# Smaller, chained GpSimd loads, key tiles zeroed by VectorE, and head pairs in the order 0, 3, 1, 2

## The chip, the cores and the metric

The kernel runs on one core of one Trainium2 chip. The metric is the device time of the whole program in microseconds (us). The kernel before takes 461.84 us, the median of three runs (461.19 to 462.41).

## The reference

Two layers follow one another. The first is a gated linear recurrence over 768 time steps for 4 batches and 8 heads of 48 channels, the second a gated two-layer product with a shift by one time step. Cut to what matters:

```python
mag = np.sqrt(a_re * a_re + a_im * a_im)
scale = np.minimum(mag, 0.999) / (mag + 1e-06)
a_re_n, a_im_n = (a_re * scale, a_im * scale)
for t in range(S):                       # S = 768, states [B, H, D, D]
    new_re = ar * S_re - ai * S_im
    new_im = ar * S_im + ai * S_re
    S_re, S_im = (new_re + k[t] (x) v[t], new_im)
    y[t] = q[t] . S_re
...
xk = mu_k * x + (1 - mu_k) * x_prev      # x: y with the heads side by side, 384 wide
xr = mu_r * x + (1 - mu_r) * x_prev
k = np.maximum(xk @ w_k, 0.0)            # 1024 wide
v = k * k @ w_v
out = sigmoid(xr @ w_r) * v
```

## The kernel before, in words

The 4 x 768 time steps are cut into 8 units of 384 steps, two for each batch (u = 0 to 7; an odd unit goes on from the state of the even one ahead of it). Each unit goes through three stages, called G, A and M here:

- **G(u)**, `gate` (L637): GpSimd loads one tile `g` of 128 x 3 x 4 x 384 numbers (three blocks of 128 channels, `ct`; in each a_re, a_im, k and q) and three tiles `v`. Unit 0's `g` is loaded by SyncE. ScalarE and VectorE then turn a_re and a_im into running logarithms and angles (L684 to L772), scale k and q (L740), and turn them by cosine and sine (L784). For unit 0 the work is done in two groups of blocks, (0) and (1, 2); for the others in one group. There are two buffers for `g`, five for `v`.
- **A(u)**, `attend` (L800): SyncE's transfers (`move`, L816) put the keys and queries of a head under each other in one of six tiles `kq`, whose rows between the real and the imaginary part hold zeros that are written once at the start (L351). TensorE multiplies keys with queries per chunk of 128 steps (`scores`, `sc`, L885), VectorE masks the product (`pt`, L889), TensorE transposes keys (`tr`, L847), updates the state (`up`, L867) and forms the outputs for pairs of heads (`y`, L908 and L915). ScalarE copies them out (`ys`, L924) and SyncE's transfers bring them into the tile `xt` (L930): pairs 0, 1 and 2 go to rows 0 to 95 of block 0, 1 and 2, pair 3 to rows 96 to 127 of all three blocks.
- **M(u)**, `mix` (L384): VectorE forms the difference of neighbouring steps (`dx`, L396) and the two mixed inputs (L405 or L415), for units other than 0 also split into a high and a low part (L423, L426). TensorE multiplies (`z`, L439 for unit 0 with whole weights, L444 for the others), ScalarE applies relu, square (L484, L488), VectorE splits again (L496), TensorE multiplies with the second weight (`o`, L512 or L515), VectorE multiplies with the sigmoid (L534) and SyncE stores. A product `z` needs all three blocks of the mixed input.

The weights come once, ten loads by GpSimd (`raw`, L363), and are decoded on ScalarE and VectorE (L578 to L588). Nineteen later loads (`again`, L627) read them a second time for a check of their range. GpSimd also copies the last step of an even unit (`last`, L947), which the odd unit's M needs.

The order of all this is written by a planner inside the kernel, the class `Plan` (L70). Every step is registered with an engine, an estimated cost, what it reads and writes, and which buffers it uses. The table `AT` (L44) gives each stage A and M a start and an end on a common scale; TensorE's steps are ordered by it and their costs added up, and each step gets a due time by walking back from those through what it feeds (`due`, L117). `run` (L156) then plays the engines forward in its own time: whenever an engine is free, it takes the step with the earliest due time among those that can start. The order so found is the order of instructions of each engine, and on the chip no engine leaves it. SyncE's transfers ("SP") and GpSimd's loads ("GP") are engines of the plan with a time per issue (`QUEUE`), and each had a data path of its own with its own rate (L325, L329). GpSimd's compute steps are booked on another engine of the plan, "POOL", though on the chip they share one stream with its loads. The line that says when transferred data is there is

```python
dma[e] = max(dma[e], t + self.START) + cost     # START 1.15, cost bytes by rate
end = dma[e] + self.ARRIVE                      # ARRIVE 0.9
```

and the head pairs are walked in the order of `PAIRS` (L46): the transfers of a pair, then its scores, then its outputs. While TensorE waits for the first M, `warm` (L962) fills it with products that nobody reads.

Of the kernel before, what the change touches and what calls it, by code (L numbers as in the profile page):

```python
# [11 lines left out]
F32 = mybir.dt.float32  # L12
# [18 lines left out]
HR = 64  # L31
# [9 lines left out]
CAP = 0.999  # L41


AT = ((0.38, 0.74), (1.0, 1.45), (1.28, 1.33), (2.34, 3.3), (2.2, 2.89), (3.4, 4.43), (3.07, 3.65), (4.24, 5.39),  # L44
      (4.34, 4.39), (4.94, 6.44), (5.25, 5.8), (7.11, 7.17), (6.14, 7.38), (7.41, 9.17), (7.2, 7.7), (9.54, 10.42))
PAIRS = 0, 1, 2, 3  # L46
PIECE = 2
GP = 2
KQ = 6
# [7 lines left out]
FIRST_LOAD = 2  # L57
# [12 lines left out]
class Plan:  # L70
# [8 lines left out]
    BEGIN = 0.8  # L79
    LATENCY = 0.16  # L80
    TABLE = 1.28
    QUEUE = dict(SP=0.63, GP=1.1)
    START, ARRIVE = 1.15, 0.9
    TURN = {("once", "half"): 0.09, ("full", "half"): 0.09,
            ("half", "once"): 0.24, ("half", "full"): 0.15}
# [70 lines left out]
    def run(self):  # L156
# [10 lines left out]
        ready = [0.0] * len(ops)  # L167
        tables = sorted(o["table"] for o in ops if o["table"])[::-1]
        table, end = None, 0.0
        dma = dict.fromkeys(self.QUEUE, 0.0)  # L170
        work = {}
        free, held, got = {}, dict.fromkeys(self.bufs, 0), dict.fromkeys(self.bufs, 0)
        taken, waiting, events, ends, order = set(), {}, [self.BEGIN], [], []
        warm = False
        kind = None

# [17 lines left out]
        while len(order) < len(ops):  # L194
            t = heapq.heappop(events) + 1e-9
            while ends and ends[0][0] <= t:
                for s in ops[heapq.heappop(ends)[1]]["uses"]:
                    users[s] -= 1
                    if not users[s]:
                        held[s[0]] -= 1  # L200
            found = True
            while found:
                found = False
                for e, queue in list(waiting.items()):
                    if free.get(e, 0.0) > t:
# [12 lines left out]
                    if self.fill and self.fill[3] in o["writes"]:  # L218
                        warm = False
                    for other in (o["engine"], *o["other"]):  # L220
                        waiting[other].discard(i)
                    if self.fill and self.fill[2] in o["writes"]:
                        warm = True
                    for tag, n in set(o["uses"]) - taken:
                        taken.add((tag, n))
                        held[tag] += 1
                        got[tag] = max(got[tag], n + 1)
                    cost = o["other"].get(e, o["cost"])
                    if o["table"]:
                        tables.pop()  # L230
                        if table != o["table"][1]:
                            table = o["table"][1]
                            cost += self.TABLE
                    if e in self.QUEUE:
                        free[e] = t + self.QUEUE[e]
                        dma[e] = max(dma[e], t + self.START) + cost
                        end = dma[e] + self.ARRIVE
                    else:
                        end = t + cost
                        if e == "PE":  # L240
                            end = t
# [29 lines left out]
def tile_kernel(ctx, tc, gat, vt, w_all, mu, slow_g, slow_v, out):  # L271
# [50 lines left out]

    def op_dma(n, f, **kw):

        plan[0].op("SP", n / 360, f, **kw)  # L325

    def op_dma_gp(n, f, **kw):

        plan[0].op("GP", n / 300, f, **kw)  # L329


    table(AF.Ln)
# [15 lines left out]

    kqs = [keep.tile([HR + D, 2, U], F32, name=f"kq{i}") for i in range(KQ)]
    for t in kqs:  # L350
        nc.gpsimd.memset(t[32:HR], 0.0)  # L351
    last = keep.tile([P, NT, 1], F32, name="last")
    nc.sync.dma_start(out=mu_sb, in_=mu)

# [188 lines left out]
    with ExitStack() as fast:  # L543
# [7 lines left out]
        slot = plan[0].slot  # L551
        G, g_slot, V, v_slot = {}, {}, {}, {}

        raws = {}

        def fetch(i):
            s = pieces[i]
# [79 lines left out]
        def gate(u):  # L637
# [6 lines left out]
            v_slot[u] = [slot("v") for _ in range(NC)]  # L644
            V[u] = []

            def load(ct, part):
                def f():
                    if u not in G:
                        G[u] = gp.tile([P, NT, 4, U], F32, tag="g", name="g")  # L650
                    (nc.gpsimd if u else nc.sync).dma_start(out=G[u][:, ct, part], in_=gat[b, half, ct, :, part])
                (op_dma_gp if u else op_dma)(196.6 * (part.stop - part.start), f, writes=[("g", u, ct, i) for i in range(part.start, part.stop)] + [("in", u, ct, part.stop)],
                       uses=[g_slot[u]])

            def load_v(c):
                def f():
                    v = ap.tile([P, C], F32, tag="v", name="v", bufs=5)
                    nc.gpsimd.dma_start(out=v, in_=vt[b, half, c])
                    V[u].append(v)
                op_dma_gp(197, f, writes=[("v", u, c)], uses=[v_slot[u][c]])  # L660

            def each(c):
                return range(c.start, c.stop)
# [126 lines left out]
                    op_dve(2 * U, lambda ct=ct: times(ct, 1), reads=[("r0", u, ct)],  # L790
                           writes=g[2:] + [("kqs", u, ct)], uses=[s_r, s_g])

            parts = (slice(0, 2), slice(2, 4)) if u < FIRST_LOAD else (slice(0, 4),)
            steps = [lambda ct=ct, part=part: load(ct, part) for part in parts for ct in cts]
            steps += [lambda c=c: load_v(c) for c in range(NC)]
            for f in (a0, a1, a2, b0, b1):
# [328 lines left out]
```

## Time and profile before

| | |
|---|---|
| median of three runs | 461.84 us |
| profiled execution | 460.59 us |
| its span, first to last instruction | 458.6 us |
| mean granted TensorE clock | 0.945 |
| bytes moved | 67.51 MB, 147 GB/s over the span |

An engine's idle time costs something only where TensorE, which does most of the work, ends up waiting for it. A row of a timeline gives start, duration, engine, source line, operation, output<-input, shape, count and, in brackets, the idle time before it with what ended that. A row of the windows gives busy time and, in parentheses, the count of instructions of each engine in a stretch, then the granted TensorE clock, the share of DMA time, and GB/s. "PEld" is TensorE's loading of weights. A row of the transfers gives their count, size and median time from issue to landing.

### The profile page before, as it was taken

The page shows a single profiled execution, that of the slowest core. Times are in us where ns is not written, and L with a number is a line of the kernel's source. Part 1 is how long each engine was busy: PE and PEld are TensorE (multiplying, and loading weights), DVE is VectorE, ACT ScalarE, POOL GpSimd, SP SyncE. Part 2 cuts the span into 40 slices and gives each one's busy share as a digit, 9 for nine tenths or more (in the row PEclk, how much of TensorE's full clock was granted, in tenths as well). Part 3 has the DMA queues.
Part 4 walks back from the last instruction along what each step waited for, and adds up shares of the span by engine and source line. Part 5 has one row for each costly group of instructions (what it writes and reads, how often), then busy time and mean ns, then how long its engine had stood idle before and what let it go on. Part 6 is the DMA issues. An engine that isn't in the chain of part 4 may idle for free.

```text
span 458.6 us, 8780 instructions
## 1 busy us (share of the span) xinstructions
PE 399.6 (87%) x3263; PEld 362.6 (79%) x3263; DVE 329.3 (72%) x536; ACT 341.6 (74%) x591; POOL 52.2 (11%) x116
## 2 busy tenths in 40 slices
PE   2005998999977999999999999999899998999994
PEld 2004995567666999999898989999799997899993
DVE  1599868669849988878886888777897866185222
ACT  5689755987768799989978799789879943563530
POOL 8510020000201120030003000011000000100000
PEclk8555999999978999999999999999999999999998
DMA  8996380602885827383647345268541455300001
GB/s 284 411 410 178 95 290 2 134 22 66 262 189 154 286 55 179 121 281 118 148 127 245 120 112 146 66 216 226 134 135 47 118 135 144 112 4 22 32 1 59
DMA packets 25074, 67.51 MB, mean 147 GB/s; under 512 B 5696, under 2 KB 11840, under 8 KB 25024
## 3 DMA queue, kind: packets, MB, share of 16 engines
q1 hardware_dynamic: 17520, 30.69, 25.6%
q0 software_dynamic: 7504, 36.18, 23.3%
q8 instruction: 28, 0.46, 0.4%
q14 instruction: 22, 0.18, 0.1%
HBM read 38.54 MB, written 4.72 MB: 94 GB/s over the span
## 4 chain that ended last, share of the span: by engine, by line
PE 56%; DMA 16%; ACT 10%; DVE 10%; issue 4%; SPq 2%; POOL 2%; DVEq 0%; ACTq 0%; POOLq 0%
PE z L444 18%; PE o L515 13%; PE sc L885 8%; DMA raw<-in_w_all 4%; DMA xt<-ys 4%; PE y L908 3%; PE o L512 3%; PE up L867 3%; DMA again<-in_w_all 3%; PE y L915 3%; PE z L439 3%; DMA kq<-g 3%; PE tr L847 2%; ACT r L295 2%; SPq L816 1%
## 5 line engine op out<-in xcount | busy, mean ns | idle before, releaser
L444 PE MATMUL z<-x,w 128*128 128x384 f32 x693 | 132.1, 340 | 0.0
L444 PEld LDWEIGHTS z<-x,w 128*128 128x128 f32 x693 | 120.6, 188 | 0.7 <-issue 0.7
L515 PE MATMUL o<-hhi,w 128*128 128x384 f32 x336 | 87.7, 342 | 0.0
L885 PE MATMUL sc<-kq 112*128 112x128 f32 x384 | 57.7, 297 | 5.8 <-DMA kq<-g 4.8
L515 PEld LDWEIGHTS o<-hhi,w 128*128 128x128 f32 x336 | 59.9, 188 | 0.6 <-issue 0.5
L885 PEld LDWEIGHTS sc<-kq 112*128 112x128 f32 x384 | 50.6, 204 | 11.0 <-issue 7.6
L515 PE MATMUL o<-hlo,w 128*128 128x384 f32 x168 | 57.1, 340 | 2.3 <-DVE hlo L496 2.2
L847 PE MATMUL tr<-ident,g 128*128 128x128 f32 x120 | 20.3, 298 | 36.2 <-DVE g L784 36.2
L847 PEld LDWEIGHTS tr<-ident,g 128*128 128x128 f32 x120 | 15.9, 153 | 39.3 <-DVE g L784 37.3
L484 ACT ACTIVATE r<-z 128x384 f32<-128x384 f32 x64 | 30.8, 483 | 20.6 <-PE z L444 20.0
L784 DVE TENSOR_TENSOR g<-g,r 128x768 f32<-128x768 f32 x48 | 43.1, 954 | 3.1 <-ACT r L295 2.9
L889 DVE TENSOR_TENSOR pt<-sc,mask 128x384 f32<-128x384 f32 x64 | 34.6, 552 | 5.4 <-PE sc L885 4.7
L515 PEld LDWEIGHTS o<-hlo,w 128*128 128x128 f32 x168 | 31.5, 188 | 3.9 <-DVE hlo L496 3.9
L423 ACT CAST x<-xm 128x384 fp32r<-128x384 f32 x42 | 21.1, 512 | 17.5 <-DVE xm L415 15.1
L488 ACT ACTIVATE h<-r 128x384 f32<-128x384 f32 x64 | 33.0, 520 | 0.8
L496 DVE TENSOR_TENSOR hlo<-h,hhi 128x384 fp32r<-128x384 f32 x56 | 30.9, 554 | 2.4 <-ACT hhi L311 1.0
L295 ACT ACTIVATE sq<-m 128x1152 f32<-128x1152 f32 (+2 forms) x27 | 28.0, 1054 | 6.1 <-DVE m L732 3.7
L908 PE MATMUL y<-pt,v 128*64 128x128 f32 (+1 forms) x384 | 29.3, 280 | 3.0 <-DVE pt L889 3.0
L311 DVE CAST hhi<-h 128x384 fp32r<-128x384 f32 x33 | 11.8, 358 | 25.9 <-PE o L515 13.4
L908 PEld LDWEIGHTS y<-pt,v 128*64 128x64 f32 (+1 forms) x384 | 20.8, 129 | 11.5 <-issue 5.8
L289 ACT ACT_TABLE_LOAD x22 | 28.2, 1283 | 1.2 <-PEq L1114 0.8
L627 POOL DMA_DIRECT2D again<-in_w_all x19 | 10.2, 539 | 161.9 <-ACT again L634 114.4
(85 smaller groups left out, 687.9 us busy)
## 6 DMA issues: line engine op xcount, KB each, us to landing
kq<-g SPq DMA_DIRECT2D x96, 144.0 KB, 3.4
g<-in_gat POOLq DMA_DIRECT2D x18, 768.0 KB, 6.4
again<-in_w_all POOLq DMA_DIRECT2D x19, 384.0 KB, 3.7
raw<-in_w_all POOLq DMA_DIRECT2D x9, 768.0 KB, 10.3
v<-in_vt POOLq DMA_DIRECT2D x24, 192.0 KB, 6.2
out_t<-y SPq DMA_DIRECT2D x24, 192.0 KB, 3.2
xt<-ys SPq DMA_DIRECT2D x48, 72.0 KB, 3.2
kq<-g SPq DMA_DIRECT2D x32, 96.0 KB, 3.1
```

Source lines behind the costliest of these rows:

```text
L289: nc.scalar.add_instruction(mybir.InstLoadActFuncSet(name=nc.get_next_instruction_name(), act_func_set_id=loaded[0], engine=mybir.EngineTy ...
L295: nc.scalar.activation(out=out, in_=in_, func=func, **kw)
L444: nc.tensor.matmul(z, lhsT=wt[s[0]][:, part, s[1]], rhs=r[which][:, ct], start=n == 0, stop=n == 3 * NT - 1)
L484: nc.scalar.activation(out=t["r", j], in_=t["f", j], func=AF.Relu)
L488: nc.scalar.activation(out=t["h", j], in_=t["r", j], func=AF.Square)
L496: nc.vector.tensor_tensor(out=t["lo", j], in0=t["h", j], in1=t["hi", j].bitcast(F32), op=ALU.subtract)
L515: nc.tensor.matmul(tiles["o", mt], lhsT=wt[W_V + 2 * j][:, part, ts(mt, P)], rhs=r, start=j == 0 and n == 0, stop=j == NJ - 1 and n == 2)
L784: nc.vector.tensor_tensor(out=g[:, ct, 2 * i:2 * i + 2], in0=g[:, ct, 2:4], in1=t["r"][:, ct, 1 - i:2 - i].to_broadcast([P, 2, U]), op=ALU ...
L847: nc.tensor.transpose(out=t["tr", c, part][:, ct * P:(ct + 1) * P], in_=G[u][:, ct, 2 * part, c * P:(c + 1) * P], identity=ident)
L885: nc.tensor.matmul(sc[:, c], lhsT=kq[h][:, 0, ts(c, P)], rhs=kq[h][:, 1, ts(c, P)], start=True, stop=True)
L889: nc.vector.tensor_mul(pts[h], t["sc", h], mask.unsqueeze(1).to_broadcast([P, NC, P]))
L908: nc.tensor.matmul(t["y", p][rows, ts(c, P)], lhsT=V[u][c][:, cols], rhs=pts[hs[j]][:, c], start=c == 0, stop=False)
```

## The change

Five things are changed together.

1. The loads of `g` come in two halves of 384 KB for every unit, first a_re and a_im of the three blocks, then k and q, where units 2 to 7 had one load of 768 KB for each block.
2. From unit 2 on, ahead of each load of `g` or `v`, GpSimd copies one number out of the tile loaded ahead of it (`touch`), and so waits until that load has landed. The planner is told of it (`reads=before(...)`).
3. The six tiles `kq` are zeroed by VectorE.
4. The planner's picture of the transfers is another: one data path for SyncE and GpSimd together, rates of 380 and 400 bytes per ns, 0.65 us per GpSimd issue, GpSimd free from 2.4 us on and VectorE from 5.5 us on.
5. `AT` and `PAIRS` have other values, so that the whole order is planned anew. In the old table A(1) lies inside M(0) and A(3) inside the end of M(1) and the start of M(2); in the new one A(1) comes after M(0), and A(2) and A(3) lie side by side in the second half of M(1).

```diff
-AT = ((0.38, 0.74), (1.0, 1.45), (1.28, 1.33), (2.34, 3.3), (2.2, 2.89), (3.4, 4.43), (3.07, 3.65), (4.24, 5.39),
-      (4.34, 4.39), (4.94, 6.44), (5.25, 5.8), (7.11, 7.17), (6.14, 7.38), (7.41, 9.17), (7.2, 7.7), (9.54, 10.42))
-PAIRS = 0, 1, 2, 3
+AT = ((1.08, 1.24), (1.06, 1.33), (1.56, 2.38), (2.41, 3.51), (2.81, 3.56), (4.05, 5.05), (2.79, 3.65), (4.94, 5.9),
+      (4.96, 5.14), (6.39, 7.0), (6.27, 6.51), (7.33, 8.26), (6.46, 8.29), (7.37, 12.32), (8.85, 9.08), (12.2, 12.46))
+PAIRS = 0, 3, 1, 2
...
-    QUEUE = dict(SP=0.63, GP=1.1)
+    QUEUE = dict(SP=0.63, GP=0.65)
+    FREE = dict(GP=2.4, DVE=5.5)
...
-                        dma[e] = max(dma[e], t + self.START) + cost
-                        end = dma[e] + self.ARRIVE
+                        dma = max(dma, t + self.START) + cost
+                        end = dma + self.ARRIVE
...
-        plan[0].op("SP", n / 360, f, **kw)
+        plan[0].op("SP", n / 380, f, **kw)
...
-        plan[0].op("GP", n / 300, f, **kw)
+        plan[0].op("GP", n / 400, f, **kw)
...
     for t in kqs:
-        nc.gpsimd.memset(t[32:HR], 0.0)
+        nc.vector.memset(t[32:HR], 0.0)
...
+            def after(key):
+
+                if loaded_by and u >= FIRST_LOAD:
+                    nc.gpsimd.tensor_copy(touch, loaded_by[-1])
+                loaded_by.append(key)
+
+            def before(key):
+                r = chain[-1:] * (u >= FIRST_LOAD)
+                chain.append(key)
+                return r
...
+                    if u:
+                        after(G[u][:1, ct, part.start, :1])
                     (nc.gpsimd if u else nc.sync).dma_start(out=G[u][:, ct, part], in_=gat[b, half, ct, :, part])
...
                     v = ap.tile([P, C], F32, tag="v", name="v", bufs=5)
+                    after(v[:1, :1])
                     nc.gpsimd.dma_start(out=v, in_=vt[b, half, c])
...
-            parts = (slice(0, 2), slice(2, 4)) if u < FIRST_LOAD else (slice(0, 4),)
+            parts = slice(0, 2), slice(2, 4)
```

More of the change, by code (lines that the diff above doesn't have):

```diff
@@ L169, in run @@
         table, end = None, 0.0
-        dma = dict.fromkeys(self.QUEUE, 0.0)
+        dma = 0.0
         work = {}
-        free, held, got = {}, dict.fromkeys(self.bufs, 0), dict.fromkeys(self.bufs, 0)
-        taken, waiting, events, ends, order = set(), {}, [self.BEGIN], [], []
+        free, held, got = dict(self.FREE), dict.fromkeys(self.bufs, 0), dict.fromkeys(self.bufs, 0)
+        taken, waiting, events, ends, order = set(), {}, [self.BEGIN, *self.FREE.values()], [], []
         warm = False
@@ L552, in tile_kernel @@
         G, g_slot, V, v_slot = {}, {}, {}, {}
-        raws = {}
+        raws, loaded_by, chain = {}, [], []
+        touch = keep.tile([1, 1], F32, name="touch")
         def fetch(i):
@@ L650, in f @@
                         G[u] = gp.tile([P, NT, 4, U], F32, tag="g", name="g")
+                    if u:
+                        after(G[u][:1, ct, part.start, :1])
                     (nc.gpsimd if u else nc.sync).dma_start(out=G[u][:, ct, part], in_=gat[b, half, ct, :, part])
-                (op_dma_gp if u else op_dma)(196.6 * (part.stop - part.start), f, writes=[("g", u, ct, i) for i in range(part.start, part.stop)] + [("in", u, ct, part.stop)],
-                       uses=[g_slot[u]])
+                key = ("in", u, ct, part.stop)
+                (op_dma_gp if u else op_dma)(
+                    196.6 * (part.stop - part.start), f, writes=[("g", u, ct, i) for i in range(part.start, part.stop)] + [key],
+                    reads=before(key), uses=[g_slot[u]])
             def load_v(c):
@@ L657, in f @@
                     v = ap.tile([P, C], F32, tag="v", name="v", bufs=5)
+                    after(v[:1, :1])
                     nc.gpsimd.dma_start(out=v, in_=vt[b, half, c])
                     V[u].append(v)
-                op_dma_gp(197, f, writes=[("v", u, c)], uses=[v_slot[u][c]])
+                op_dma_gp(197, f, writes=[("v", u, c)], reads=before(("v", u, c)), uses=[v_slot[u][c]])
             def each(c):
```

## The prediction

> **What bounds the kernel now.** I read the page first, then the busy times by stage, then for each stage where TensorE stands still the waits, the timeline and the chain.
>
> ```profile
> span 458.6 us, 8780 instructions
> PE 399.6 (87%) x3263; PEld 362.6 (79%) x3263; DVE 329.3 (72%) x536; ACT 341.6 (74%) x591; POOL 52.2 (11%) x116
> PE 56%; DMA 16%; ACT 10%; DVE 10%; issue 4%; SPq 2%; POOL 2%; DVEq 0%; ACTq 0%; POOLq 0%
> ```
>
> TensorE is the busiest engine, yet a sixth of the chain is transfers. The stretches say where; I cut them at the points where TensorE's work changes (start, A(0), the way to M(0), M(0) with A(1), A(2), the long middle).
>
> ```profile
> core 0: us, PE busy (x) PEld busy (x) DVE busy (x) ACT busy (x) POOL busy (x), PEclk, DMA share, GB/s
> 0.00:35.60 35.60, 2.93 (x12) 2.64 (x12) 20.26 (x32) 24.19 (x42) 17.90 (x44) 0.62 0.95 368
> 35.60:40.20 4.60, 0.48 (x2) 0.19 (x2) 4.57 (x8) 4.58 (x6) 0.00 (x0) 0.50 0.63 165
> 40.20:61.10 20.90, 20.90 (x259) 19.31 (x259) 18.97 (x28) 15.65 (x27) 2.02 (x4) 0.85 0.54 148
> 61.10:81.30 20.20, 18.24 (x104) 13.73 (x102) 13.73 (x21) 11.40 (x17) 1.77 (x4) 1.00 0.31 109
> 81.30:125.00 43.70, 43.67 (x309) 29.84 (x310) 35.18 (x44) 37.87 (x58) 3.19 (x6) 1.00 0.45 122
> 125.00:150.00 25.00, 18.71 (x214) 16.33 (x212) 16.67 (x30) 16.95 (x27) 2.12 (x4) 0.80 0.74 171
> 150.00:447.00 297.00, 289.85 (x2343) 276.07 (x2344) 216.73 (x374) 230.99 (x418) 25.17 (x55) 1.00 0.45 128
> ```
>
> From 150 us on TensorE is idle for 297.00 - 289.85 = 7.15 us in all: there it is the bound, and no order of the work brings more than that. What can be won lies in front: 40.2 us until TensorE's work starts, the way from A(0) to M(0), and 125 to 150, where it is idle for 6.29 us and the granted clock is 0.80 (by the clock alone 25.00 x 0.20 = 5.0 us more).
>
> **The start.** The waits and the timeline of the first 45 us:
>
> ```profile
> PE tr L847 <- DVE g L784: 34.9, 2, 30.8
> ```
>
> ```profile
> 2.27 4.11 POOL L351 MEMSET kq<- 32x768 f32 x6
> 4.47 0.52 ACT L684 ACTIVATE m<-g 128x384 f32<-128x384 f32 x1 [2.37 <-DMA g<-in_gat]
> 6.32 1.74 POOL L651 DMA_DIRECT2D g<-in_gat  x3
> 6.80 0.84 ACT L684 ACTIVATE m<-g 128x768 f32<-128x768 f32 x1 [1.09 <-DMA g<-in_gat]
> 8.18 0.56 DVE L690 SCALAR_TENSOR_TENSOR ph<-ph,g 128x384 f32<-128x384 f32 x1 [7.22 <-ACT ph L295]
> 15.73 0.56 ACT L578 ACTIVATE raw<-raw 128x384 int32<-128x384 uint8 x1 [5.02 <-DMA raw<-in_w_all]
> ```
>
> TensorE waits for G(0), and in the middle of G(0) ScalarE stands still for 5.02 us: the planner put the decoding of the first weights there because in its picture GpSimd's loads have a path of their own, and the weights came late. With one shared path they are expected later, and G(0)'s next steps take that place. I count 5.0 us off. Against it: GpSimd no longer zeroes the tiles (4.11 us), so its loads set out at about 2.3 instead of 6.32 us and share the path with unit 0's blocks 1 and 2, which land between 4.47 and 6.80 us; at half the rate these 2.33 us become 4.66, so at most 2.3 us later. I take 1.5, since the first half of that stretch passes before GpSimd's data flows. The zeroing on VectorE costs nothing: it has 7.22 us of idle time before 8.18, and six tiles of 768 columns take 3.3 to 5.7 us there by the two nearest rows of that width:
>
> ```profile
> L784 DVE TENSOR_TENSOR g<-g,r 128x768 f32<-128x768 f32 x48 | 43.1, 954 | 3.1 <-ACT r L295 2.9
> ...
> L732 DVE TENSOR_SCALAR m<-m 128x768 f32<-128x768 f32 x1 | 0.6, 554 | 0.0
> ```
>
> If that cover were gone it would be those us. **Term 1: -3.5 us** (bounds -5.0 and +2.3).
>
> **From A(0) to M(0).**
>
> ```profile
> 61.12 8.30 PE L966 MATMUL warm<-mask,ident 128*128 128x128 f32 x72
> 70.88 9.91 PE L439 MATMUL z<-x,raw 128*128 128x384 f32 x30 [1.45 <-issue]
> ```
>
> ```profile
> 67.88 0.56 DVE L396 TENSOR_TENSOR dx<-xt 128x384 f32<-128x384 f32 x1 [3.00 <-DMA xt<-ys]
> ...
> 70.17 1.67 DVE L405 SCALAR_TENSOR_TENSOR x<-dx,mu_sb,xt 128x384 f32<-128x384 f32 x3
> 71.75 2.83 DVE L751 TENSOR_TENSOR_SCAN ph<-ph,stat,consts 128x384 f32<-128x384 f32 x3
> ```
>
> ```profile
> 61.99 2.43 SPq L930 DMA_DIRECT2D xt<-ys  x4
> ```
>
> TensorE fills 8.30 us with products that nobody reads and is idle for 1.45, because all three blocks of `xt` wait for pair 3, the last: four transfers of 2.43 / 4 = 0.61 us each, then the differences and the mixed inputs of three blocks. In the order 0, 3, 1, 2 block 0 is whole after two pairs and block 1 after three; behind the last pair come two transfers and one block. That takes two transfers (1.2 us) and, for two blocks, 2 x (0.56 + 2 x 0.56) = 3.4 us of VectorE out of the way: 4.6 us, if VectorE does them under A(0), where it is busy for 18.97 of 20.90 us. I take 4.0. Less than nothing is hardly possible, as no step is added; the upper bound is the whole of 20.20 - 9.91 = 10.3 us, if G(1)'s scans (2.83 us, in the middle of that work) also move behind, which the later place of A(1) in the table favours. **Term 2: -4.0 us** (0 to -10.3).
>
> **The stall of A(2).**
>
> ```profile
> 115.29 1.58 POOL L651 DMA_DIRECT2D g<-in_gat  x3 [45.00 <-ACT r L772]
> ```
>
> ```profile
> 121.96 8.43 DMA kq<-g
> ```
>
> ```profile
> 128.78 3.31 PE L885 MATMUL sc<-kq 112*128 112x128 f32 x12 [3.46 <-DMA kq<-g]
> ```
>
> ```profile
> kq<-g SPq DMA_DIRECT2D x96, 144.0 KB, 3.4
> g<-in_gat POOLq DMA_DIRECT2D x18, 768.0 KB, 6.4
> again<-in_w_all POOLq DMA_DIRECT2D x19, 384.0 KB, 3.7
> ```
>
> The chain holds a transfer of keys of 8.43 us where the median is 3.4, and ahead of it stand G(3)'s three loads, issued in 1.58 us. Chained, one load of 384 KB is under way instead of 2.3 MB, and the transfer is 8.43 - 3.4 = 5.0 us earlier; TensorE's idle 6.3 us and the low clock, which follows it, shrink with that. Also in the new table M(1) stands ahead of A(2) and can fill. I take half of 6.3 + 5.0 = 11.3, since A(2)'s late readiness has a second cause, G(2)'s own end. **Term 3: -5.5 us** (0 to -11.3). A rule of the Trainium skill, DMA: Bandwidth & Descriptors, section Queues, rings and completion order, says that each DMA engine takes turns between the queues packet by packet; by it a bulk load of any size costs a transfer beside it half the rate and no more, so size alone would not help, only the pauses between the links. No row of this trace shows the turns.
>
> **The middle.** Of the 7.15 us from 150 on I take a fifth, as TensorE is the bound and other steps will be late instead. **Term 4: -1.5 us** (+3 to -7).
>
> **The chain of loads.** Each unit from 2 on has six loads of 384 KB and three of 192 KB one behind the other. A link takes issue to landing, 3.7 us for 384 KB by the row above and 3.2 for 192 KB by the stores, plus the copy of one number, at most the 0.9 us that a copy of `last`, three numbers in 128 rows, takes:
>
> ```profile
> out_t<-y SPq DMA_DIRECT2D x24, 192.0 KB, 3.2
> ```
>
> ```profile
> L947 POOL COPY last<-xt 128x3 f32<-128x3 f32 x4 | 3.6, 901 | 22.4 <-DMA xt<-ys 14.7 <-DMA kq<-g 6.4 <-issue 1.2
> ```
>
> 6 x 3.7 + 3 x 3.2 = 31.8 us, with the copies up to 31.8 + 9 x 0.9 = 39.9. What is there to cover it, in unit 4 of before:
>
> ```profile
> 147.87 1.58 POOL L651 DMA_DIRECT2D g<-in_gat  x3 [6.66 <-DMA out_t<-y]
> ```
>
> ```profile
> 165.34 1.17 ACT L684 ACTIVATE m<-g 128x1152 f32<-128x1152 f32 x1
> ```
>
> ```profile
> 185.10 2.17 PE L867 MATMUL up<-v,kt 128*64 128x48 f32 x64
> ```
>
> G(4) begins 17.5 us after its loads set out; the first three links, a_re and a_im, are there after 11.1 to 13.8 us. The last `v` is there after 31.8 to 39.9 us, and `up` wants it 185.10 - 147.87 = 37.2 us after the start: the cover is there, but used up to the edge. The planner books a link of 384 KB with 393 / 400 + 1.15 + 0.9 + 0.16 (its latency) = 3.2 us and one of 192 KB with 2.7, 27.3 us for nine; the rows say 31.8 and the copies, so that GpSimd runs 4.5 us or more behind its plan by the last link. Behind a waiting copy are queued, in GpSimd's one stream, the next loads of `g` and `v`, the loads of `again` (nobody but the range check waits for them) and the copy `last`, for which the odd unit's M waits. Six units of 31.8 us fit into the 300 us from 150 us on, so the path as a whole is not full. I charge 0.5 us for each of six units. **Term 5: +3.0 us** (0 to +27, below). A second rule of the Trainium skill, DMA: Bandwidth & Descriptors, section Rules for kernel authors, speaks against the change: at least 1 MiB for a transfer. By that page's fit, 2.0 us and the bytes at 436 GB/s, the nine links would take 6 x 2.9 + 3 x 2.45 = 24.8 us, an estimate, instead of 31.8; term 5 would then be near 0. The trace's link of 384 KB, 3.7 us, is slower than that fit.
>
> The rest has one answer: the count of steps, table loads and matmuls is the same, and the end behind the last product (unit 7's stores) is untouched.
>
> **Sum.** -3.5 - 4.0 - 5.5 - 1.5 + 3.0 = -11.5 us. The profiled execution took 460.59 us (its span and 2.0 us around it), so 449.1; it lies 1.25 us under the median of the runs, which makes 461.84 - 11.5 = **450.3 us**.
>
> **Rivals.**
>
> *VectorE bounds the start, and the gain is handed back.* For it:
>
> ```profile
> 20.00:30.00 10.00, 0.00 (x0) 0.00 (x0) 9.98 (x16) 9.21 (x16) 3.42 (x5) 0.50 1.02 412
> ```
>
> VectorE is full there; ScalarE's 5.02 us may only uncover that. Against it: much of what VectorE does in that stretch is decoding of weights, which has time until M(0). Terms 1 and 2 would be 0: 461.84 - 5.5 - 1.5 + 3.0 = **457.8 us**. Chance 0.13.
>
> *The transfers share anyway, so A(2) still stalls.* Keys and loads would move in turns whatever the size of a load. For it: the bytes are the same. Against it: three loads issued in 1.58 us keep the path full for most of the 8.43 us, a chained one, 0.39 MB at the 412 GB/s of the row above, for 0.96 of its 3.7 us. This is the rule of the Trainium skill on turns between queues, named above, made a mechanism of this kernel. Term 3 would be 0: 461.84 - 6.0 = **455.8 us**. Chance 0.10.
>
> *The chain is late (slower).* One place: the last links of each unit, k, q and `v`. They come 31.8 - 27.3 = 4.5 us later than planned, and every engine keeps the planned order, so TensorE stands at `up` or at the scores. If all of it lands on TensorE in six units: 6 x 4.5 = 27 us in term 5's place, 461.84 - 14.5 + 27 = **474.3 us**. It decides from 14.5 / 6 = 2.4 us for each unit on. For it: the cover of 37.2 us against 31.8 to 39.9. Against it: G(u) has two buffers, and where TensorE is full for 30 us on end it is behind the plan as well. Chance 0.24.
>
> *More is won.* Terms 2 and 3 at their ends: 461.84 - 11.5 - 6.3 - 5.8 = **438.2 us**. Chance 0.07, as both stretches would have to close wholly.
>
> **How the numbers follow.** The forecast has 0.46, with a range of its own from 443 to 457 (terms 1 to 4 half again as large, or half as large). The whole range, 441 to 466, takes in the two weaker gains and the mild part of the late chain, and leaves out most of that case and of the last. About 0.3%, 1.4 us, is what a measurement can tell from no change. Faster by more than that: 0.44 of the forecast's 0.46, 0.09 of 0.13, 0.09 of 0.10, 0.07, and 0.02 of the late chain, in sum 0.71. Within it: 0.05, from the weaker gains. Slower: 0.24, the late chain for the most part.
>
> **What would show it.** Right, step by step: no wait of ScalarE for `raw` in the first 30 us and the first `tr` at 35 to 37 us, with TensorE's steady work from about 36.5 instead of 40.2 (term 1); fewer than 8.30 us of `warm` ahead of the first `z` and less than 10 us between A(0)'s last output and M(0) without gaps (term 2); no transfer of keys over 6 us and a clock of 1.00 from 110 to 150 us (term 3); under 7 us idle from 150 us to the last product (term 4); no wait of TensorE that goes back to `v` or `g` (term 5). Wrong: TensorE waiting for `up` or `tr` behind GpSimd's loads in several units, or ScalarE at L684 waiting for `g` for over 2 us in each; a start of TensorE's work at 40 us or later with VectorE full; or a stretch of half clock after 60 us at another place, which would mean that the stall only moved.

## The result, and the profile after

| | before | after |
|---|---|---|
| median | 461.51 us (four runs) | 497.06 us (four runs, 494.31 to 498.73) |
| ratio | 1 | 1.0773, 95% interval 1.0708 to 1.0838 |
| profiled execution, span | 460.59, 458.6 us | 497.66, 496.0 us |

The change makes the kernel slower by 36 us, where 450.3 us was forecast and 466 was the upper end of the range. Most lines of the kernel moved by 1 to 18: `again` is now loaded at L629 and read at L633 (VectorE) and L635 (ScalarE), `touch` is L652, the loads of `g` and `v` are L666 and L676, `m` is L702, `y` L926 and L933, `state` L890, `ys` L942.

The head of the page of after, with the busy times and the shares of the chain that ended last:

```profile
span 496.0 us, 8829 instructions
...
PE 408.9 (82%) x3247; PEld 370.5 (75%) x3247; DVE 332.5 (67%) x545; ACT 341.3 (69%) x588; POOL 84.9 (17%) x182
...
PE 50%; DMA 30%; DVE 7%; issue 4%; ACT 3%; POOL 3%; SPq 1%; POOLq 0%; DVEq 0%; ACTq 0%
```

TensorE's idle time went from 458.6 - 399.6 = 59.0 to 496.0 - 408.9 = 87.1 us, which is 28.1 of the 37.4 us of span; the other 9.3 us are nearly the same work (3247 matmuls instead of 3263) taking longer. Transfers hold 30% of the chain instead of 16%. The busy times of after by stage, cut at the same events as before:

```profile
core 0: us, PE busy (x) PEld busy (x) DVE busy (x) ACT busy (x) POOL busy (x), PEclk, DMA share, GB/s
0.00:36.80 36.80, 3.88 (x14) 3.00 (x14) 27.34 (x42) 28.87 (x47) 13.51 (x38) 1.00 0.95 366
36.80:57.90 21.10, 20.84 (x259) 18.93 (x259) 18.96 (x29) 14.54 (x24) 0.54 (x1) 1.00 0.58 121
57.90:64.10 6.20, 6.20 (x56) 6.20 (x57) 6.20 (x12) 5.36 (x7) 4.02 (x3) 1.00 0.20 56
64.10:84.00 19.90, 11.97 (x35) 6.75 (x35) 10.06 (x13) 8.36 (x12) 6.61 (x9) 0.87 0.33 84
84.00:127.00 43.00, 43.00 (x304) 29.32 (x303) 34.03 (x45) 35.94 (x58) 6.28 (x11) 0.98 0.53 120
127.00:150.00 23.00, 16.12 (x204) 14.49 (x204) 13.45 (x25) 12.59 (x24) 3.87 (x9) 0.85 0.82 185
150.00:486.00 336.00, 303.80 (x2370) 289.12 (x2366) 220.07 (x382) 235.60 (x420) 50.03 (x113) 0.94 0.45 117
```

The start is won as forecast (36.8 instead of 40.2 us). From 150 us on TensorE is idle for 336.00 - 303.80 = 32.2 us instead of 7.15, at a mean clock of 0.94 instead of 1.00; from 64 to 84 us it is idle for 7.9. So nearly the whole loss is in the middle, the stretch that was called full. The waits of after name who stands, for whom, and how long (total us, times, longest us):

```profile
POOL touch L652 <- DMA g<-in_gat: 140.8, 36, 7.1
...
DVE again L633 <- DMA again<-in_w_all: 42.3, 12, 10.9
...
POOL touch L652 <- DMA v<-in_vt: 33.4, 14, 4.4
...
ACT again L635 <- DVE again L633: 32.7, 9, 9.5
...
PE y L933 <- DVE state L890: 15.9, 2, 8.6
...
ACT m L702 <- DMA g<-in_gat: 15.8, 5, 8.8
...
PE o L513 <- ACT h L489: 7.9, 1, 7.9
...
PE y L926 <- ACT ys L942: 5.7, 1, 5.7
```

GpSimd stands 174 us at `touch`, as the change means it to. What was not foreseen is the second line: VectorE stands 42.3 us, up to 10.9 at a time, for the loads of the range check. The same wait in before:

```profile
DVE again L631 <- DMA again<-in_w_all: 18.5, 10, 5.4
```

The timeline of one of these places in after, where every row carries its engine, reads as a chain of queues:

```profile
245.73 0.45 POOL L652 COPY touch<-g 1x1 f32<-1x1 f32 x1 [7.12 <-DMA g<-in_gat]
246.20 0.54 POOL L666 DMA_DIRECT2D g<-in_gat  x1
...
250.07 0.17 POOL L652 COPY touch<-g 1x1 f32<-1x1 f32 x1 [3.33 <-DMA g<-in_gat]
250.54 0.54 POOL L676 DMA_DIRECT2D v<-in_vt  x1 [0.30 <-PE y L933]
...
253.30 0.17 POOL L652 COPY touch<-v 1x1 f32<-1x1 f32 x1 [2.23 <-DMA v<-in_vt]
...
253.77 0.54 POOL L676 DMA_DIRECT2D v<-in_vt  x1 [0.30 <-issue]
...
254.31 0.54 POOL L629 DMA_DIRECT2D again<-in_w_all  x1
...
258.01 0.59 DVE L633 TENSOR_SCALAR again<-again 128x384 uint8<-128x384 uint8 x1 [10.94 <-DMA again<-in_w_all]
...
258.40 0.58 DVE L890 TENSOR_TENSOR state<-up,state 112x384 f32<-112x384 f32 x1
...
259.03 0.69 PE L933 MATMUL y<-kq,state 112*64 112x128 f32 x4 [8.61 <-DVE state L890]
```

GpSimd is through `touch` after `touch` only at 254.31 us, and only then issues the load of `again`. VectorE has its step of the range check next in its order and stands 10.94 us for it. Behind that step, on VectorE, is the update of `state`, a step of 0.58 us whose input was ready, and TensorE stands 8.61 us for that update. The same happens at 312.48 us (the load of `again`; TensorE then stands 5.7 us, by way of ScalarE's `again` and `ys`) and at 368.75 us (7.25 us, by way of `state`). The granted clock is 0.75 between 244 and 262 us, 0.77 between 310 and 325 and 0.73 between 374 and 384, so each of the three stalls costs more than its length.

### The profile page after: what moved, and what is told of

Its sections match the earlier page's. It is cut to its first block, busy times and chain, and to the rows that moved or that the text cites. A ratio compares the mean times of both kernels' runs of the same rounds, so it can differ in the third digit from the quotient of the medians.

```text
span 496.0 us, 8829 instructions
## 1 busy us (share of the span) xinstructions
PE 408.9 (82%) x3247; PEld 370.5 (75%) x3247; DVE 332.5 (67%) x545; ACT 341.3 (69%) x588; POOL 84.9 (17%) x182
## 4 chain that ended last, share of the span: by engine, by line
PE 50%; DMA 30%; DVE 7%; issue 4%; ACT 3%; POOL 3%; SPq 1%; POOLq 0%; DVEq 0%; ACTq 0%
DMA g<-in_gat 20%; PE z L445 17%; PE o L516 11%; PE sc L903 8%; DMA v<-in_vt 4%; PE y L926 4%; DMA again<-in_w_all 3%; PE y L933 3%; POOL touch L652 2%; PE o L513 2%; PE z L440 2%; PE up L885 2%; DMA kq<-g 2%; PE tr L865 2%; DMA xt<-ys 1%
## 5 line engine op out<-in xcount | busy, mean ns | idle before, releaser
L445 PE MATMUL z<-x,w 128*128 128x384 f32 x693 | 136.5, 348 | 0.0
L445 PEld LDWEIGHTS z<-x,w 128*128 128x128 f32 x693 | 124.3, 194 | 1.2 <-issue 1.2
L903 PE MATMUL sc<-kq 112*128 112x128 f32 x384 | 59.3, 303 | 11.0 <-DMA kq<-g 4.8
L903 PEld LDWEIGHTS sc<-kq 112*128 112x128 f32 x384 | 52.1, 210 | 17.3 <-issue 6.5
L633 DVE TENSOR_SCALAR again<-again 128x384 uint8<-128x384 uint8 x19 | 11.6, 609 | 47.7 <-DMA again<-in_w_all 42.3
L652 POOL COPY touch<-g 1x1 f32<-1x1 f32 x36 | 19.0, 529 | 140.8 <-DMA g<-in_gat 140.8
L865 PEld LDWEIGHTS tr<-ident,g 128*128 128x128 f32 x120 | 16.2, 156 | 34.5 <-DVE g L802 33.1
L933 PE MATMUL y<-kq,state 112*48 112x128 f32 (+1 forms) x320 | 25.7, 282 | 15.9 <-DVE state L890 15.9
L926 PE MATMUL y<-pt,v 128*64 128x128 f32 (+1 forms) x384 | 30.6, 288 | 6.2 <-ACT ys L942 5.7
L635 ACT ACTIVATE again<-again,consts 128x384 f32<-128x384 uint8 x19 | 12.4, 654 | 32.7 <-DVE again L633 32.7
L926 PEld LDWEIGHTS y<-pt,v 128*64 128x64 f32 (+1 forms) x384 | 22.0, 134 | 14.4 <-ACT ys L942 6.0
L933 PEld LDWEIGHTS y<-kq,state 112*48 112x48 f32 (+1 forms) x320 | 20.4, 134 | 16.4 <-DVE state L890 16.3
```

The source lines that it names most:

```text
L445: nc.tensor.matmul(z, lhsT=wt[s[0]][:, part, s[1]], rhs=r[which][:, ct], start=n == 0, stop=n == 3 * NT - 1)
L652: nc.gpsimd.tensor_copy(touch, loaded_by[-1])
L865: nc.tensor.transpose(out=t["tr", c, part][:, ct * P:(ct + 1) * P], in_=G[u][:, ct, 2 * part, c * P:(c + 1) * P], identity=ident)
L903: nc.tensor.matmul(sc[:, c], lhsT=kq[h][:, 0, ts(c, P)], rhs=kq[h][:, 1, ts(c, P)], start=True, stop=True)
L926: nc.tensor.matmul(t["y", p][rows, ts(c, P)], lhsT=V[u][c][:, cols], rhs=pts[hs[j]][:, c], start=c == 0, stop=False)
L933: nc.tensor.matmul(t["y", p][rows, ts(c, P)], lhsT=st[:, cols], rhs=kq[hs[j]][:, 1, ts(c, P)], start=False, stop=c == NC - 1)
```

## The experiments

My theory after the result: the waits of `touch` are the loss, and most of it goes through the check loads queued behind them. The rivals: the size of the loads, the new order, the zeroing, or the pairs. "Order kept" means below that every engine's instructions stand in the order of the kernel from which the experiment is made and only what the diff shows differs; "replanned" means that the planner wrote a new order.

**After without the waits** (order kept):

```diff
-                if loaded_by and u >= FIRST_LOAD:
-                    nc.gpsimd.tensor_copy(touch, loaded_by[-1])
```

> The changed kernel with its planned order kept on every engine, but without the 50 copies of one number, so that GpSimd no longer waits for a load to land. Theory A (the waits themselves cost the time: GpSimd runs late, ScalarE stands at g, VectorE at the range check's loads queued behind the chain, and TensorE behind both): the stalls go and the time falls from 497 to 450-460 us. Rival B (the new table, pair order and planner model give a worse order whatever GpSimd does): it stays above 480 us. Rival C (smaller loads contend more with the key transfers): about 475-490 us, with key transfers at 5 us or more.

Measured: 462.79 us, 1.0051 of before (1.0014 to 1.0089), 3 us above the range of theory A. (The trace of after has 54 copies, of which 50 waited.) The waits and their copies cost 497.1 - 462.8 = 34 us. All else, the halves, the new order, the zeroing and the pairs together, makes the kernel no faster: it is 2 us slower than before.

**After, its copies reading something that is always there** (order kept):

```diff
-                    nc.gpsimd.tensor_copy(touch, loaded_by[-1])
+                    nc.gpsimd.tensor_copy(touch, mask[:1, :1])
```

> The changed kernel with every order kept, in which the copy of one number reads the mask instead of the tile loaded ahead, so that the 50 copies are there and nothing is waited for. If the waits cost the time: 461-465 us, like the kernel without the copies (462.8). If the copies themselves or VectorE's shared use of memory with GpSimd cost it: 475 us or more.

Measured: 465.4 us (461.67 to 472.09), 1.0119 (1.0055 to 1.0182). Its interval overlaps that of the run without copies, so the copies themselves cost at most a few us; the waiting is the rest, 29 to 34 us by that interval.

**After, with the check's loads issued by ScalarE** (order otherwise kept):

```diff
-                nc.gpsimd.dma_start(out=raw.bitcast(I32), in_=w_all[:, i * C:(i + 1) * C].bitcast(I32))
+                nc.scalar.dma_start(out=raw.bitcast(I32), in_=w_all[:, i * C:(i + 1) * C].bitcast(I32))
```

> The changed kernel, but the 19 loads of the range check are issued by ScalarE instead of GpSimd, at the same place of the plan, so that they no longer queue behind the chain. If VectorE's waits for them (42.3 us in all, and through the state update 15.9 us of TensorE, 5.7 us through ys) are the main way the chain costs time: 470-478 us. If the waits of ScalarE for g are the main way: 490 us or more.

Measured: 465.27 us, 1.0097 (1.0064 to 1.0129): the waits of `touch` are still there, and 32 of the 36 us are gone, 5 more than the expectation's best. Its waits, in the same columns:

```profile
POOL touch L652 <- DMA g<-in_gat: 141.6, 36, 6.8
...
ACT m L702 <- DMA g<-in_gat: 14.1, 4, 8.8
...
DVE again L633 <- DMA again<-in_w_all: 9.6, 6, 3.3
...
PE o L513 <- ACT h L489: 7.8, 1, 7.8
```

GpSimd waits for `g` as long as in after (141.6 against 140.8 us); VectorE's wait for `again` fell from 42.3 to 9.6 us. TensorE's waits for `state` and `ys` behind those loads, 15.9 + 5.7 us in after, are gone. What the chain of loads still costs here is ScalarE at the head of G(2), 8.8 us, with TensorE behind it, 7.8 us, and ScalarE at the head of G(3), 6.6 us. The edit does two things at once: the check's loads no longer come late, and GpSimd no longer stands for their buffer (34.7 + 16.1 + 10.9 = 61.7 us in after), with the loads of `g` and `v` queued behind. The three stalls above are of the first kind; the 32 us hold both.

**Both: no waits, and the check's loads on ScalarE** (order otherwise kept; the two diffs above together).

> The changed kernel's order without the waits (462.8 us) and with the range check's loads issued by ScalarE (which was worth 31.8 us with the waits and 1.8 us in the kernel before). Theory A: once nothing waits behind a chain the place of those loads hardly matters, 459-463 us. If the order itself still loses through those loads: 455 us or less.

Measured: 448.79 us (six runs), 0.9758 (0.9728 to 0.9788). The place of those loads matters after all, against theory A. This beats both kernels by 12 and 48 us. Its page and its stages:

```profile
span 446.0 us, 8723 instructions
...
PE 395.0 (89%) x3247; PEld 359.2 (81%) x3247; DVE 333.1 (75%) x545; ACT 340.6 (76%) x588; POOL 47.1 (11%) x109
```

```profile
36.00:60.00 24.00, 22.56 (x264) 20.41 (x264) 19.45 (x30) 14.71 (x26) 0.89 (x2) 1.00 0.55 113
60.00:80.00 20.00, 19.31 (x94) 13.44 (x94) 17.54 (x24) 15.03 (x19) 4.80 (x9) 1.00 0.56 176
80.00:125.00 45.00, 39.87 (x296) 27.34 (x294) 35.77 (x48) 35.81 (x59) 4.78 (x9) 0.98 0.55 136
125.00:150.00 25.00, 23.27 (x269) 21.56 (x270) 16.13 (x31) 19.08 (x34) 1.08 (x2) 0.90 0.68 160
150.00:436.00 286.00, 282.46 (x2297) 270.10 (x2296) 213.83 (x369) 226.78 (x407) 22.30 (x50) 1.00 0.46 130
```

From 150 us on TensorE is idle for 3.5 us and the clock is 1.00 again; from 60 to 80 it is idle for 0.7 us, where after has its 7.9.

**The same in the old order.** Three kernels from before, order kept: the waits alone, with the loads of 768 KB left whole; the check's loads alone; both.

```diff
-                    (nc.gpsimd if u else nc.sync).dma_start(out=G[u][:, ct, part], in_=gat[b, half, ct, :, part])
+                    u and after(G[u][:1, ct, part.start, :1]); (nc.gpsimd if u else nc.sync).dma_start(out=G[u][:, ct, part], in_=gat[b, half, ct, :, part])
...
-                    nc.gpsimd.dma_start(out=v, in_=vt[b, half, c])
+                    after(v[:1, :1]); nc.gpsimd.dma_start(out=v, in_=vt[b, half, c])
```

> The kernel before, every engine's order kept and the loads whole, with only the copy of one number ahead of each load of units 2 to 7 (six links of a unit, three of 768 KB and three of 192 KB). Theory A, that GpSimd's waits alone cost it: 475-495 us, as the loads of g and v then land 10 us and more later and the range check's loads queue behind them. Rival: the chain costs only together with the order planned for it: under 468 us.

> The kernel before with the 19 loads of the range check issued by ScalarE. VectorE waits 18.5 us for them in the kernel before, of which the chain shows one 4.9 us piece: 457-460 us if those waits reach TensorE, 461 us if they are covered.

> The kernel before with the waits on whole loads, every other order kept (492.8 us), and the range check's loads issued by ScalarE. If those loads behind the waits are most of the cost in the old order as in the new one (31.8 of 34): 462-470 us. If ScalarE's and VectorE's waits for g itself are most of it: 480-490 us.

Measured: 492.81 us, 1.0693 (1.0656 to 1.073); 459.62 us, 0.9964 (0.9934 to 0.9994); 466.5 us, 1.0172 (1.0121 to 1.0223). Waits of the first:

```profile
DVE again L631 <- DMA again<-in_w_all: 50.0, 13, 9.9
```

and of the third:

```profile
ACT m L684 <- DMA g<-in_gat: 19.3, 4, 8.3
...
DVE again L631 <- DMA again<-in_w_all: 13.8, 6, 5.7
```

With the kernels above this makes two tables of four, medians in us (the before kernel's own medians beside them were 460.1 to 461.5):

| | check loads by GpSimd | by ScalarE |
|---|---|---|
| old order, no waits | 460.6 (before) | 459.6 |
| old order, waits | 492.8 | 466.5 |
| new order, no waits | 462.8 | 448.8 |
| new order, waits | 497.1 (after) | 465.3 |

The waits cost 32 and 34 us where the check's loads stand behind them, and 7 and 16 where they don't, in either order. So it is not the new order that makes them dear. By difference, 25 of the 32 us in the old order and 18 of the 34 in the new one come by way of the check's loads. Moving those loads gains 32 us in after, but 14 of these it gains without the waits too. The remaining 16 us of the new order fit ScalarE's stands for `g` at G(2) and G(3), with TensorE behind them; that the 7 us of the old order are its waits for `g` (19.3 us, against 6.6 in before) is argued, not shown.

**Size alone, zeroing alone** (from before, order kept): each 768 KB load as two halves one right after the other; the six tiles zeroed by VectorE.

```diff
-                    (nc.gpsimd if u else nc.sync).dma_start(out=G[u][:, ct, part], in_=gat[b, half, ct, :, part])
+                    [(nc.gpsimd if u else nc.sync).dma_start(out=G[u][:, ct, i:i + 2], in_=gat[b, half, ct, :, i:i + 2]) for i in range(part.start, part.stop, 2)]
```

```diff
-        nc.gpsimd.memset(t[32:HR], 0.0)
+        nc.vector.memset(t[32:HR], 0.0)
```

> The kernel before, every order kept, each load of g of units 2 to 7 issued as two halves one right after the other, with no wait. Size alone: 460-463 us, the same as before. If smaller loads by themselves free the key transfers: 458 us or less; if the second issue on GpSimd costs: 464 us or more.

> The kernel before, every order kept, with the six tiles zeroed by VectorE: GpSimd's loads set out at about 2.2 instead of 6.3 us. The planned anew form of this took 469.4 us. If that loss came from planning anew: 458-461 us here, with the stall of ScalarE at the first weights shorter by 2 to 4 us. If it came from the loads colliding with unit 0's: 464 us or more.

Measured: 462.7 us, 1.0073 (1.0041 to 1.0106), and 460.96 us, 1.0015 (0.9984 to 1.0045). Smaller loads cost 2 us when nothing else is changed; the zeroing costs and brings nothing. The same from the other side, the fastest kernel with the zeroing given back to GpSimd (order kept):

> The fastest kernel so far (changed order, no waits, check loads by ScalarE, 448.8 us) with the zeroing back on GpSimd, order kept. The first loads set out 4.1 us later than planned. If the zeroing on VectorE is worth its place in the plan: 450-454 us. If the start is bound by VectorE: 449 us, no difference.

Measured: 448.97 us, 0.976 (0.9724 to 0.9797), against 448.79. TensorE's steady work begins at 36.65 us, with the zeroing on VectorE at 35.76 us. The zeroing is worth at most these 0.9 us, and two traces with the same zeroing and the same order up to there differ as much (35.76 here, 36.84 in after): the earlier start is not due to the zeroing in the main.

**Parts alone, replanned.** From before: the halves, the waits and the planner's knowledge of them (the blocks `after` and `before` of the change); the same with the check's loads on ScalarE; the zeroing with `FREE = dict(GP=2.4, DVE=5.5)` in the plan; `PAIRS = 0, 3, 1, 2`. All with the old table `AT`.

> The kernel before with the chain alone: halves for units 2 to 7, the copy ahead of each load and the planner told of it; table, pair order, planner model and zeroing as before. Theory A: slower than before by 10 to 35 us (471 to 497 us), with VectorE and ScalarE waiting for the loads of the range check and of g. Rival B: within 5 us of before (457 to 467 us), as the chain has cover.

> The kernel before with the chain (as in the run of the chain alone, 498 us) and with the range check's loads issued by ScalarE. If those loads behind the chain are what costs nearly all of it, in the old order too: 461-468 us. If the wait of ScalarE for g is what costs it in the old order: 485 us or more.

> The kernel before, with the six tiles zeroed by VectorE and the planner told when GpSimd (2.4 us) and VectorE (5.5 us) are free; table, pairs, loads and the rest of the planner as before. If term 1's offset was right and the ScalarE stall at the first weights comes from the separate paths in the plan, the weights set out 4.1 us earlier and the stall shrinks by 2 to 4 us: 457-460 us. If VectorE bounds the start: 460-462 us, no change.

> The kernel before with only the pair order 0, 3, 1, 2, planned anew. Term 2 says about 4 us less (456-458 us), as block 0 and 1 of xt are whole before the last pair. The rival, that VectorE is full under A(0) and G(1) takes the freed place, says 460-463 us.

Measured: 498.22 us, 1.0856 (1.0783 to 1.093); 488.19, 1.0549 (1.048 to 1.0617); 469.35, 1.0169 (1.0122 to 1.0216); 479.45, 1.0387 (1.0323 to 1.0451). The first lies 1 us above the range of its theory. The second was meant to repeat the recovery and gave back only 10 us, as its other case said: VectorE's wait for `again` fell to 6.6 us, but ScalarE stands for `g` for 23.6 us. The third and fourth lie outside both of their ranges and can't be read as the cost of their part. The zeroing costs nothing where the order is kept, and 8 us where it is replanned. For the pairs, one row of the timeline of TensorE shows that replanning changed more than the pairs: the new order has the scores of the first keys ahead of all else, and TensorE waits for these keys.

```profile
40.69 1.62 PE L885 MATMUL sc<-kq 112*128 112x128 f32 x6 [35.87 <-DMA kq<-g]
```

This costs only 0.5 us (the steady work begins at 40.69 instead of 40.20); from 150 us on TensorE is idle for 16.2 us instead of 7.15. What in the plan led to that was not traced.

**After without the chain in the plan either, replanned** (`before` returns nothing, no copies; then with the check's loads on ScalarE too):

```diff
-                r = chain[-1:] * (u >= FIRST_LOAD)
+                r = []
```

> The changed kernel without the chain in program and plan (halves, zeroing, planner model, table and pair order kept), planned anew. Theory A: 448-460 us, faster than before by the gains of the start and of the way to M(0). Rival B (table tuned for another plan, or worse order): 465 us or more.

> The changed kernel planned without the chain (472.0 us) with the range check's loads issued by ScalarE. If the order that was planned with the chain in mind is itself what gains (448.8 us), this stays above 455 us. If the gain comes from the new planner model and zeroing alone, 446-452 us.

Measured: 471.95 us, 1.0241 (1.0213 to 1.0269), and 465.68 us, 1.0147 (1.0099 to 1.0196). Against the kernels whose order was planned with the chain and run without it, 462.8 and 448.8, they are 9 and 17 us slower. With the zeroing and the pairs above, that makes four replannings that each lost 8 to 18 us, so a table `AT` seems to suit one exact plan. The 12 us of the fastest kernel come with the order that was planned for spread loads and the move of the check's loads together: that order alone gives 462.8, the move alone 459.6.

## Why the prediction was wrong, point by point

**Term 5, the chain of loads, is the step that failed**: +3.0 us forecast, +34 measured (after against after without the waits), which is over its upper bound of +27 too. Two readings in it were wrong. The first is the list of what is queued behind a waiting copy. Of the loads of `again` it says: "nobody but the range check waits for them". That is true of the data and false of the engines. The range check's reader is a step of VectorE in a fixed order, and the update of `state` stands behind it. TensorE stands 15.9 + 5.7 us that way, and by the table 18 of the 34 us come through those loads (25 of 32 in the old order).

The second is the cover, which was read from unit 4 and taken for all six. Units 2 and 3 don't have it. ScalarE stands 8.84 us at the head of G(2) and 7.83 us at the head of G(3); in before it stood 0 and 3.15 us there. Without the waits these two steps begin at 70.54 and 127.02 us, with them at 77.73 and 140.12:

```profile
140.12 1.16 ACT L702 ACTIVATE m<-g 128x1152 f32<-128x1152 f32 x1 [7.83 <-issue]
...
140.17 0.17 POOL L652 COPY touch<-g 1x1 f32<-1x1 f32 x1 [5.15 <-DMA g<-in_gat]
```

The first row names no releaser ("issue"), but it begins as the third link of G(3) lands, for which the copy of the second row had waited.

Of the link's length the prediction had the direction and too small a size: in unit 5's chain, the six loads of `g` took from 219.40 us (the issue of the first) to 250.07 us (the copy that ends the sixth), 30.7 us or 5.1 each, where the planner books 3.2 and the prediction 3.7 and up to 0.9 for the copy. (The 0.9 is the mean of four copies of `last`, not the most that one takes: one took 2.19 us.) That is 30.7 - 6 x 3.2 = 11.5 us more than the plan has for these six links. VectorE's 10.94 us at 258 us are near it, but that they are the same us was not shown.

The rival "the chain is late" named the cause. Its place, `v`, k and q at `up` and the scores, is not where TensorE stood for the most part, and its 27 us came from one wait per unit. The loss is three stalls of 5.7 to 8.6 us behind the check's loads, one of 7.9 us behind G(2), one of 4.1 us behind G(3) (term 3 below), and the low clock. The sign that the prediction gave for it, ScalarE standing for `g` for over 2 us in several units, shows in two of six. (Of the 15.8 us of `m` above, 2.67 + 2.94 are unit 0's, whose loads SyncE issues.)

**Term 1, the start**: -3.5 forecast; TensorE's steady work begins at 36.84 instead of 40.20, -3.4, and ScalarE no longer stands for `raw`. The size is right. That it comes from the new order and not from the zeroing is shown by the kept-order runs: with the old order and VectorE's zeroing the steady work begins at 39.83 us, with the new order and GpSimd's at 36.65. Unit 0's blocks 1 and 2 came 2.2 us later (ScalarE's L684 step begins at 6.80 us before, its L702 at 8.96 after), near the bound of 2.3 and over the 1.5 taken.

**Term 2, the way from A(0) to M(0)**: -4.0 forecast. From A(0)'s last output to the first `z`, before took 70.88 - 61.12 = 9.8 us, after 64.16 - 57.80 = 6.4, -3.4. Then the chain took it back: G(2)'s first half came late, ScalarE stood 8.84 us at its first step and M(0)'s `h` behind that, so that the first `o` began at 81.93 us, against 81.33 before. The timeline of after:

```profile
77.73 1.16 ACT L702 ACTIVATE m<-g 128x1152 f32<-128x1152 f32 x1 [8.84 <-DMA g<-in_gat]
...
81.93 2.29 PE L513 MATMUL o<-h,raw 128*128 128x384 f32 x3 [7.93 <-ACT h L489]
```

Without the waits and with the check loads moved, the first `o` begins at 76.16 us: terms 1 and 2 together bring 5.2 us of the forecast 7.5. Whether the pairs did it was not settled; the one run of them alone was replanned.

**Term 3, the stall of A(2)**: -5.5 forecast, and in after nothing came of it: TensorE is still idle for 6.9 us from 127 to 150 us, at a clock of 0.85. Yet its mechanism is borne out in part. With every order kept, TensorE's waits for keys between 80 and 150 us are 5.7 us without the waits of `touch` and 1.5 with them (6.9 and 1.2 with the check's loads on ScalarE; before, 3.5). What filled the place is the chain itself: 4.1 of the 6.9 us are spent behind a copy of transposed keys (`kt`) that stands on ScalarE behind G(3)'s late `m`:

```profile
PE sc L903 <- ACT kt L871: 4.1, 1, 4.1
```

Over the whole run the transfers of keys became slower, not faster. The issues of after (count, size, median us to landing):

```profile
g<-in_gat POOLq DMA_DIRECT2D x42, 384.0 KB, 4.2
kq<-g SPq DMA_DIRECT2D x96, 144.0 KB, 5.0
again<-in_w_all POOLq DMA_DIRECT2D x19, 384.0 KB, 3.8
...
v<-in_vt POOLq DMA_DIRECT2D x24, 192.0 KB, 2.7
```

Their median went from 3.4 to 5.0 us. With the order kept, the waits alone move it from 4.6 to 5.0 us, and from 3.6 to 5.4 with the check's loads on ScalarE. The link issued at 127.10 us, beside them, took 6.51 us, where those issued at 63.34 and 70.15 us took 3.46 and 3.55. By the Trainium skill, DMA: Bandwidth & Descriptors, section Queues, rings and completion order, each DMA engine takes turns between queues packet by packet; the higher medians don't contradict it, but no row shows the turns. In the fastest kernel, whose loads come in bursts again, TensorE is idle for 5.1 + 1.7 = 6.9 us from 80 to 150 us, before for 6.3: the stall moved and only the clock there is better. So the term wasn't realised, and the rival of 455.8 us, that keys stall whatever the size of a load, isn't what happened either. (That rival's 0.96 us is 0.95 by its own numbers.)

**Term 4, the middle**: -1.5 forecast. In after TensorE is idle for 32.2 us there, instead of 7.15. In the fastest kernel it is idle for 3.5, which is -3.6.

Terms 1 to 4 are -14.5 us in sum. The change without its waits shows +2. Its first `o` begins at 75.09 instead of 81.33 us, but over the run TensorE stands 17.4 us for keys, against 4.8 before:

```profile
PE sc L903 <- DMA kq<-g: 17.4, 7, 5.6
```

So of the 47 us between the forecast and the result some 31 are term 5's and some 16 are gains of terms 1 to 4 that the change does not bring. The fastest kernel has -11.8 us, near the -14.5, but with the check's loads on ScalarE, which is no part of the change; that the two numbers are near each other is luck.

The clue for term 5 was in the view that the prediction had read: before, VectorE already waited 18.5 us, ten times, for `again`, the largest of its waits. A load for which a working engine stands today has no slack, whatever its data is for.

What stays open: moving the check's loads brings 1 us in the old order and 14 in the new one without waits. In the kernel without waits, its check loads still on GpSimd, the waits show GpSimd standing for their buffer, with the loads of `g` and `v` queued behind:

```profile
POOL again L629 <- ACT again L636: 88.5, 9, 17.3
```

TensorE's 17.4 us for keys in that kernel compare with 9.5 in the fastest one. That the two belong together was not tried, and before has the same wait of GpSimd, 114.4 us, where moving the loads brought 1 us.

## What to carry to other kernels

A wait on an engine that works in order delays everything queued behind it; list each queued thing, then the engine that reads it, then what stands behind that reader on its engine, until the list ends at the bound. Read the cover for every unit, not for one. "Only a side task waits for it" is no end of that list. Where a planner writes the order, test a part with the order kept first: here replanned runs mixed each part's cost with 8 to 18 us of planning.

## What the runs showed of the hardware

A copy of one number by GpSimd took 0.17 to 3.3 us (mean 0.53 for those out of `g`), the two longest early, at 60 and 67 us. The group of the page of after (total us, mean ns, idle time before):

```profile
L652 POOL COPY touch<-g 1x1 f32<-1x1 f32 x36 | 19.0, 529 | 140.8 <-DMA g<-in_gat 140.8
```

Between its end and the issue of the next link lie up to 0.3 us more in most cases, and 0.7 us at most where GpSimd waits for no buffer in between. Links of 192 KB landed after a median of 2.7 us, less than the 3.2 taken from the stores. By the Trainium skill, DMA: Bandwidth & Descriptors, section Anatomy of one DMA — SWDGE (gpsimd) path, 2.0 us and the bytes at 436 GB/s, six links of 384 KB would be 6 x 2.9 = 17.4 us, an estimate; the 30.7 us above disagree with it; transfers of keys and a load of `again` went beside the links in that stretch. VectorE zeroed the six tiles in 4.74 us, GpSimd in 4.11.
